# Folding four more blocks of an out-projection, with the row moves issued by GpSimd

## The chip, the cores and the metric

The kernel runs on one core of a Trainium2 chip. The metric is the device time of one execution in microseconds (us), the median of several runs. Engines are named as in the profile: PE is TensorE (PEld its weight loads), DVE is VectorE, ACT is ScalarE, POOL is GpSimd, SP is SyncE, which here only issues transfers.

## The reference

Four layers follow each other on `x` of 2048 tokens by 448 numbers (bf16): attention, gated MLP, attention, gated MLP. Each adds to `x` what it computes from the layer-normed `x`.

```
def _A_ref(x, wqkv, wo):                      # 16 heads of 28, window of 8 keys, two tokens apart
    q, k, v = split(x @ wqkv)
    logits = q . k[pos - 2*(0..7)] * 28**-0.5     # masked where the position is negative
    o = softmax(logits) @ v
    return o.reshape(B, S, 448) @ wo              # the out-projection
def _B_ref(x, w_gate, w_up, w_down):
    return ((x @ w_gate) * (x @ w_up)) @ w_down   # 448 -> 1792 -> 448
x = x + _A_ref(layernorm(x), A_wqkv, A_wo);  x = x + _B_ref(layernorm(x), ...)
x = x + _A_ref(layernorm(x), A_wqkv, A_wo);  x = x + _B_ref(layernorm(x), ...)
```

## The kernel before

Tokens lie in 16 blocks of 128 (even tokens first, then odd ones). The layers are numbered 0 to 3; 0 and 2 are attention, 1 and 3 the MLP. Everything stays in SBUF; attention and MLP of neighbouring layers overlap, chunk by chunk.

**Work on PE.** The matmuls of the projections contract 64 rows at a time, and two of them run side by side on the two halves of PE's rows. Such a *pair* is two rows of the profile that start together (helper `pair`, line L353: 64 rows, 128 columns of weights, 256 to 512 columns of data). Scores (L838) and attention times V (L873) are bursts of many small matmuls, 64 rows by 32 columns (64 by 64 in the first groups). Between the halves of a burst, a pair may be written as eight strips of 32 columns (line L356, tiles `64*32`), so that PE keeps its small shape through the burst.

**Out-projection.** `attn_back` makes the attention outputs of 120 tokens, `norm` (L901 to L914) divides by the softmax sum and writes `oT`: 16 heads stand in 512 rows (4 chunks of 128), each head 28 rows and 4 pad rows. `y_blocks(li, B)` multiplies two blocks B and B+1 with `wo_g` by `twin_blocks`: 8 pairs, or 16 matmuls, in two parts of 4 pairs each. `x_block` (DVE, L946) adds the result to `x_sb`.

**Fold.** 448 of the 512 rows hold numbers. For blocks from `FOLD[li]` on, the last two heads (rows 64 to 127 of chunk 3) are moved by DMA into the pad rows of the other chunks: four moves `mv`, 3 or 4 rows by 4 rows, 512 or 1024 bytes each, then one move `mw` that copies rows 0 to 63 of chunk 3 of the odd blocks to rows 64 to 127, since the second block of a pair needs them on the other half. Seven pairs are then enough. The weights are folded once in the same way (`wf` 0 to 3 from DRAM, then `wf` 4 within SBUF), after the last unfolded out-projection and before the first folded one. In layer 2 all blocks are folded, in layer 0 those from 10 on. `GROUPS` says how many blocks share one set of moves.

**Order.** Nothing is scheduled at run time. `ORDER` gives, for each engine, the numbers of the operations one after the other, and `BANKS` the PSUM banks; both are tables that were found by a search outside of the file. An entry `a+b*c` means that bursts a and b are cut up between strips of operation c. `emit` puts a semaphore wait ahead of an operation that needs another engine's result; what stands behind it on the same engine waits too. Transfers are issued by SP in the order of its row (`plain_dma`, L446, and the transposes L608 and L735).

Of the kernel before, what the change touches and what calls it, by code (L numbers as in the profile page):

```python
# [8 lines left out]
D = 448  # L9
H = 16  # L10
DH = 28
# [3 lines left out]
NBLK = S // 128  # L15
NCH = S // 512
QB = 120
NQB = 17
# [15 lines left out]
FOLD = {0: 10, 2: 0}  # L34
# [63 lines left out]
def grp_nc(g):  # L98
# [56 lines left out]
    ),  # L155
    "pool": (
        "24 18 28 29 25 39 40 32 33 35 41 26 20 22 21 30 27 36 19 31 34 42 37 43 44 68 66 38 77 23 76"
    ),
# [223 lines left out]
def build(nc, A_x, A_wqkv, A_wo, B_w_gate, B_w_up, B_w_down, out):  # L382
# [10 lines left out]
    bf = dt.bfloat16  # L393
# [524 lines left out]
    def y_blocks(li, B, prio):  # L918
        bk = Banks(2)
# [208 lines left out]
```

## Time and profile before

| | |
|---|---|
| median of 3 runs | 380.81 us (380.18 to 380.89) |
| the profiled execution | 380.47 us, span 378.7 us |
| PE busy | 373.6 us, 99% of the span |
| DVE, ACT, POOL busy | 285.4, 200.0, 7.8 us |
| granted clock of PE | 1.00 |
| matmuls on `wo_g` in whole pairs (L353) | 228 rows, 349 ns each |
| transfers `oT<-oT` issued by SP | 40, median 638 ns of SP each |

A matmul's row in the profile is longer than the step to the next one, since matmuls are pipelined: what a pair costs is read from the start of one row of the timeline to the start of the next, not from the duration of an instruction. The timeline's rows name start, length, engine, line and operation, the tiles as out<-in with partitions x elements, the count, and in brackets the idle time before. In the list of waits a row gives engine, line and tile, what it waited for, and then the total in us, the number of times and the longest.

### The profile page before, as it was taken

What the parts mean: (1) busy time and instruction counts of PE and PEld (TensorE: products, weight loads), DVE (VectorE), ACT (ScalarE), POOL (GpSimd) and SP (SyncE); (2) the same over time, 40 slices, a digit from 0 to 9 for tenths busy, and PEclk for the clock granted to TensorE, in tenths of its full rate; (3) what the DMA queues carried; (4) which work ended last, traced back from release to release, by engine and by line L of the source; (5) the groups of instructions that cost most, each with busy time, mean ns of one, the idle gap of its engine ahead of it and who ended that gap; (6) DMA issues with size and microseconds to landing.
All of it is one profiled execution on the core that took longest, in us unless ns stands there. A gap on an engine that the chain in (4) does not pass through costs nothing.

```text
span 378.7 us, 14371 instructions
## 1 busy us (share of the span) xinstructions
PE 373.6 (99%) x6376; PEld 208.7 (55%) x6376; DVE 285.4 (75%) x647; ACT 200.0 (53%) x384; POOL 7.8 (2%) x35
## 2 busy tenths in 40 slices
PE   8999999999999999999999999999999999999997
PEld 3645577644554445544676666645555444445764
DVE  7998999999867953878698598559699778446324
ACT  4897895778715355246548215638647533043310
POOL 6000000000000000000000000000000000000000
PEclk9999999999999999999999999999999999999999
DMA  7665544500250216312104123510106102312002
GB/s 260 167 163 144 112 113 95 81 10 13 31 86 5 58 28 93 43 28 50 25 10 64 27 29 63 93 31 5 29 12 102 35 5 54 74 42 70 2 2 85
DMA packets 56401, 23.10 MB, mean 61 GB/s; under 512 B 46004, under 2 KB 56324, under 8 KB 56340
## 3 DMA queue, kind: packets, MB, share of 16 engines
q1 hardware_dynamic: 56196, 22.14, 28.1%
q8 instruction: 50, 0.82, 0.9%
q14 instruction: 11, 0.09, 0.1%
q10 hardware_dynamic: 144, 0.06, 0.1%
HBM read 8.59 MB, written 2.71 MB: 30 GB/s over the span
## 4 chain that ended last, share of the span: by engine, by line
PE 96%; ACT 2%; POOL 1%; DVE 1%; issue 0%; DVEq 0%; POOLq 0%
PE ps L353 86%; PE ps L356 4%; PE ps L838 2%; PE ps L873 2%; PE ps L997 1%; POOL hT L493 1%; ACT E_sb L848 1%; PE ps L619 0%; PE ps L515 0%; ACT xnTa L626 0%; ACT qk L715 0%; DVE Qz L826 0%; PE ps L615 0%; ACT v_sb L807 0%; ACT xnTa L629 0%
## 5 line engine op out<-in xcount | busy, mean ns | idle before, releaser
L353 PE MATMUL ps<-xnTb,WGU 64*128 64x512 bf16 (+1 forms) x1898 | 173.3, 332 | 0.0
L353 PEld LDWEIGHTS ps<-xnTb,WGU 64*128 64x128 bf16 x1898 | 91.4, 94 | 71.2 <-DVE hT L985 0.6
L982 ACT ACTIVATE g_sb<-ps 128x512 bf16<-128x512 f32 (+1 forms) x140 | 68.9, 509 | 92.4 <-PE ps L353 88.4
L985 DVE TENSOR_TENSOR hT<-g_sb,ps 128x512 bf16<-128x512 bf16 (+1 forms) x140 | 77.4, 573 | 38.2 <-ACT g_sb L982 37.3
L353 PE MATMUL ps<-WD,hT 64*128 64x448 bf16 x786 | 80.8, 349 | 0.0
L353 PEld LDWEIGHTS ps<-WD,hT 64*128 64x128 bf16 x786 | 37.4, 94 | 32.4 <-DVE hT L985 0.2
L353 PE MATMUL ps<-xnTa,WQK 64*128 64x512 bf16 (+1 forms) x490 | 52.1, 352 | 0.0
L946 DVE TENSOR_TENSOR x_sb<-x_sb,ps 128x448 bf16<-128x448 bf16 x62 | 36.6, 611 | 16.4 <-PE ps L353 16.3
L848 ACT ACTIVATE E_sb<-ps,shift_sb 128x1024 bf16<-128x1024 f32 (+1 forms) x36 | 37.9, 1071 | 14.2 <-PE ps L838 13.8
L605 DVE TENSOR_SCALAR xn_sb<-x_sb,mv,rstd 128x896 bf16<-128x896 bf16 (+1 forms) x64 | 35.0, 568 | 6.6 <-ACT rstd L589 5.8
L584 DVE BATCH_NORM_STATS2 st<-x_sb 128x6 f32<-128x448 bf16 x64 | 38.5, 615 | 1.0 <-DMA x_sb<-in_A_x_dram 0.7
L353 PEld LDWEIGHTS ps<-xnTa,WQK 64*128 64x128 bf16 x490 | 23.1, 94 | 20.9 <-DVE WQK L523 0.3
L715 ACT ACTIVATE qk<-ps 128x1024 bf16<-128x1024 f32 (+1 forms) x28 | 25.4, 931 | 14.2 <-PE ps L353 12.0
L902 ACT ACTIVATE R_sb<-R_sb 128x480 f32<-128x480 f32 (+1 forms) x34 | 20.4, 603 | 13.7 <-DVE R_sb L901 13.6
L855 DVE TENSOR_TENSOR E_sb<-E_sb,MK 128x1024 bf16<-128x1024 bf16 (+1 forms) x36 | 23.4, 655 | 4.6 <-ACT E_sb L848 4.6
L914 DVE TENSOR_TENSOR oT<-O_sb,R_sb 128x480 bf16<-128x480 f32 (+5 forms) x38 | 22.2, 600 | 5.3 <-ACT R_sb L903 5.3
L353 PE MATMUL ps<-wo_g,oT 64*128 64x448 bf16 x228 | 25.6, 349 | 0.0
L353 PE MATMUL ps<-WV,xnTa 64*128 64x336 bf16 (+3 forms) x252 | 23.0, 304 | 0.6 <-DVE O_sb L891 0.2
L901 DVE STREAM_SHUFFLE R_sb<-O_sb 128x480 f32<-128x480 f32 (+1 forms) x34 | 23.2, 691 | 0.0
L826 DVE TENSOR_SCALAR Qz<-qk,qmask 128x960 bf16<-128x960 bf16 (+1 forms) x36 | 14.7, 451 | 7.5 <-ACT qk L715 6.5
L903 ACT ACTIVATE R_sb<-R_sb 128x480 f32<-128x480 f32 (+1 forms) x34 | 20.0, 602 | 0.4
L587 ACT ACTIVATE lnv<-mv,eps_sb 128x2 f32<-128x2 f32 (+2 forms) x31 | 8.9, 293 | 19.1 <-DVE mv L586 19.1
(63 smaller groups left out, 221.0 us busy)
## 6 DMA issues: line engine op xcount, KB each, us to landing
out_dram<-x_sb SPq DMA_DIRECT2D x15, 112.0 KB, 1.8
x_sb<-in_A_x_dram SPq DMA_DIRECT2D x3, 448.0 KB, 5.6
hT<-in_A_wqkv_dram SPq DMA_DIRECT2D x4, 224.0 KB, 4.6
WGU<-in_B_w_gate_dram SPq DMA_DIRECT2D x4, 224.0 KB, 3.7
WGU<-in_B_w_up_dram SPq DMA_DIRECT2D x4, 224.0 KB, 4.3
WD<-in_B_w_down_dram SPq DMA_DIRECT2D x2, 448.0 KB, 4.0
WGU<-in_B_w_gate_dram SPq DMA_DIRECT2D x2, 336.0 KB, 4.6
WGU<-in_B_w_up_dram SPq DMA_DIRECT2D x2, 336.0 KB, 4.6
```

Source lines behind the costliest of these rows:

```text
L353: return lambda E: E.matmul(out(), lhs(), rhs(), start=start, stop=stop)
L584: sc.add("dve", one(lambda E, B=B: E.bn_stats(st6[:, B, :], x_sb[:, B, :]), ("bn", li, B)), 525.0, deps=[("x", li - 1, B)] + ([("xn", li - ...
L605: sc.add("dve", one(lambda E, B=B, dst=dst, src=src: E.tensor_scalar(dst, src, mv[:, B, 0:1], rstd[:, B:B + 1], ALU.subtract, ALU.mult), ( ...
L715: return E.activation(dst, src, ACT.Copy) if hasattr(E, "activation") else E.tensor_copy(dst, src)
L848: return E.activation(E_sb[:, slot, 2 * hp:2 * hp + 2, 0:w], ps[:, b0:b0 + 2, 0:w], ACT.Exp, bias=shift_sb[:, 0:1], scale=SCALE)
L855: return E.tensor_tensor(e, e, MK[:, kind, 0:nc].unsqueeze(1).unsqueeze(1).to_broadcast([128, 2, w // nc, nc]), ALU.min)
L901: sc.add("dve", one(lambda E: E.stream_shuffle(R_sb[:, rs, 0:w], O_sb[:, os_, 0:w], [DH] * 32), ("Rs", li, qb)), dve_est(w) + 20.0, deps=[ ...
L902: sc.add("act", one(lambda E: E.activation(R_sb[:, rs, 0:w], R_sb[:, rs, 0:w], ACT.Ln), ("Rl", li, qb)), act_est(w, False), deps=[("Rs", l ...
L914: return E.tensor_tensor(oT[:, :, (a + 256) % HALF:(a + 256) % HALF + z - a], O[:, :, a - tok:z - tok], R_sb[:, rs, 0:w].rearrange("p (h n ...
L946: sc.add("dve", one(lambda E: E.tensor_tensor(x_sb[:, B, :], x_sb[:, B, :], ps[:, bk[w], 0:D], ALU.add), ("x", li, B)), dve_est(D), deps=[ ...
L982: sc.add("act", one(lambda E, gs=gs, bk=bk: E.activation(g_sb[:, gs, 0:nt], ps[:, bk[0], 0:nt], ACT.Copy), ("G", li, j, fc)), act_est(nt), ...
L985: sc.add("dve", one(lambda E, gs=gs, bk=bk, fc=fc: E.tensor_tensor(hT[:, fc, hs, 0:nt], g_sb[:, gs, 0:nt], ps[:, bk[1], 0:nt], ALU.mult), ...
```

## The change

`FOLD` for layer 0 goes from 10 to 6, so blocks 6 to 9 (two more calls of `y_blocks`) take 7 pairs in place of 8. The moves `mv`, `mw` and `wf` are issued by POOL (`"pool"` in place of `"sp"`). `mw` writes to a new tile `oU` in place of rows 64 to 127 of `oT`, and therefore waits for the attention outputs and for two of the four `mv` (before, it waited for all four); the out-projection waits for all five. The tables `ORDER` and `BANKS` are new: up to the first attention groups of layer 0 they are as they were, behind that they differ on every engine.

```diff
-FOLD = {0: 10, 2: 0}
+FOLD = {0: 6, 2: 0}
...
+    oU = sb([128, 4, 128], bf, "oU")
...
             if B == G:
                 a = 128 * ((B + 2) % 8)
                 for j, row, m, _, _ in PADS:
-                    plain_dma("sp", oT[32 * j + DH:32 * j + 32, 0:m, a:a + 128 * n], oT[row:row + 4 * m, 3, a:a + 128 * n], ("mv", li, B, j), f"d_m{li}_{B}", deps=norms(B, B + n), prio=prio - 0.1)
-                odd = [oT[lo:lo + 64, 3, a:a + 128 * n].rearrange("p (b w) -> p b w", w=256)[:, :, 128:256] for lo in (64, 0)]
-                plain_dma("sp", odd[0], odd[1], ("mw", li, B), f"d_m{li}_{B}", deps=[("mv", li, B, j) for j in range(4)], prio=prio - 0.1, mode=1)
-            nd = nd + [("mw", li, G)]
+                    plain_dma("pool", oT[32 * j + DH:32 * j + 32, 0:m, a:a + 128 * n], oT[row:row + 4 * m, 3, a:a + 128 * n], ("mv", li, B, j), f"d_{'mw'[j > 1]}{li}_{B}", deps=norms(B, B + n), prio=prio - 0.1)
+                odd = [oU[64:128, a // 256:a // 256 + n // 2, :], oT[0:64, 3, a:a + 128 * n].rearrange("p (b w) -> p b w", w=256)[:, :, 128:256]]
+                plain_dma("pool", odd[0], odd[1], ("mw", li, B), f"d_w{li}_{B}", deps=norms(B, B + n) + [("mv", li, B, 0), ("mv", li, B, 1)], prio=prio - 0.1, mode=1)
+            nd = nd + [("mw", li, G)] + [("mv", li, G, j) for j in range(4)]
...
-                    plain_dma("sp", wo_g[32 * j + DH:32 * j + 32, 0:m, :], ...
-                plain_dma("sp", wo_g[64:128, 3, :], wo_g[0:64, 3, :], ("wf", 4), "d_wf", ...
+                    plain_dma("pool", wo_g[32 * j + DH:32 * j + 32, 0:m, :], ...
+                plain_dma("pool", wo_g[64:128, 3, :], wo_g[0:64, 3, :], ("wf", 4), "d_wf", ...
...
     "pool": (
-        "24 18 28 29 25 39 40 32 33 35 41 26 20 22 21 30 27 36 19 31 34 42 37 43 44 68 66 38 77 23 76"
+        "24 18 28 29 25 39 40 32 33 35 41 26 20 22 21 30 27 36 19 31 34 42 37 43 44 68 66 38 77 23 76 432 430 429 431 424 433 425 426 427 428 564 561 562 563 "
...
```

Three places of the new order follow.

POOL, which issued no transfer before, at the moves of blocks 10 to 13 of layer 0 (rows of the changed kernel; `oT<-oT` are `mv`, `oU<-oT` is `mw`; the brackets name the semaphores waited for, `sem_dve` here for the attention outputs):

```order
L447 DMA oT<-oT 4x4x256 [waits sem_dve]
L447 DMA oT<-oT 4x4x256
L447 DMA oT<-oT 4x4x256 [waits sem_dve]
L447 DMA oU<-oT 64x128 [waits sem_d_m0_10]
L447 DMA oT<-oT 4x3x256
L447 DMA oT<-oT 4x4x256
L447 DMA oT<-oT 4x3x256 x2
L447 DMA oU<-oT 64x128 [waits sem_d_m0_12]
L447 DMA oT<-oT 4x3x256
```

The moves of blocks 12 and 13 are mixed into those of 10 and 11: the third row waits for the later outputs, and the eight transfers from there on stand behind that wait. On SP the same moves stood, in the kernel before, as follows:

```order
L446 DMA wo_g<-wo_g 64x448 [waits sem_d_wf]
L446 DMA oT<-oT 4x3x256 [waits sem_dve]
L446 DMA oT<-oT 4x4x256 x2
L446 DMA oT<-oT 64x128 [waits sem_d_m0_10]
L446 DMA oT<-oT 4x3x256
L446 DMA oT<-oT 64x128 [waits sem_d_m0_12]
```

PE, at the out-projections that need these moves (rows of the changed kernel from the last of a stretch of MLP down-projections, `WD,hT`, on):

```order
L353 MATMUL ps<-WD,hT 128x448 x56
L353 MATMUL ps<-xnTb,WGU 128x512 x84
L353 MATMUL ps<-wo_g,oT 128x448 x7
L353 MATMUL ps<-wo_g,oU 128x448
L353 MATMUL ps<-wo_g,oT 128x448 x7
L353 MATMUL ps<-wo_g,oU 128x448
L353 MATMUL ps<-wo_g,oT 128x448 x12
L353 MATMUL ps<-xnTb,WGU 128x512 x56
```

The two out-projections, of blocks 12 and 10, now stand together behind 84 MLP matmuls; before, 56 down-projection and 56 MLP matmuls preceded them, and MLP matmuls lay between their parts.

PE, at a place near the front, before:

```order
L873 MATMUL ps<-E_sb,v_sb 32x64 x32
L353 MATMUL ps<-xnTb,WGU 128x256 x28
L873 MATMUL ps<-E_sb,v_sb 32x64 x32
L353 MATMUL ps<-xnTb,WGU 128x256 x56
L353 MATMUL ps<-wo_g,oT 128x448 x8
```

and in the changed kernel:

```order
L874 MATMUL ps<-E_sb,v_sb 32x64 x64
L353 MATMUL ps<-xnTb,WGU 128x256 x84
L353 MATMUL ps<-wo_g,oT 128x448 x8
L353 MATMUL ps<-xnTb,WGU 128x256 x14
L353 MATMUL ps<-wo_g,oT 128x448 x8
```

Two bursts with MLP pairs between them became one burst.

More of the change, by code (lines that the diff above doesn't have):

```diff
@@ L138 @@
         "148 166 154 183 161 184 167 45 185 165 163 156 157 46 151 210 170 188 173 159 73 78 172 71 74 72 75 190 191 179 246 193 215 181 176 216 178 251 270 219 "
[16 rows of a table removed]
[16 rows of a table added]
     ),
     "pool": (
-        "24 18 28 29 25 39 40 32 33 35 41 26 20 22 21 30 27 36 19 31 34 42 37 43 44 68 66 38 77 23 76"
+        "24 18 28 29 25 39 40 32 33 35 41 26 20 22 21 30 27 36 19 31 34 42 37 43 44 68 66 38 77 23 76 432 430 429 431 424 433 425 426 427 428 564 561 562 563 "
+        "565 590 591 648 594 593 649 651 592 652 650 680 678 679 677 681 844 847 846 845 848 997 996 999 998 1000 1217 1216 1218 1219 1220 1404 1403 1401 1402 "
+        "1405 1454 1455 1458 1457 1456"
     ),
     "sp": (
[7 rows of a table removed]
[5 rows of a table added]
     ),
@@ L433, in build @@
     sem_names += [f"d_t{li}_{j}" for li in range(4) for j in range(len(CH[li]))]
-    sem_names += [f"d_p{li}_{j}" for li in (0, 2) for j in range(len(CH[li]))] + [f"d_v{q}" for q in range(NQB)] + ["d_one", "d_stv", "d_wf"] + [f"d_m{l}_{b}" for l in (0, 2) for b in range(0, NBLK, 2)]
+    sem_names += [f"d_p{li}_{j}" for li in (0, 2) for j in range(len(CH[li]))] + [f"d_v{q}" for q in range(NQB)] + ["d_one", "d_stv", "d_wf"] + [f"d_{k}{l}_{b}" for k in "mw" for l in (0, 2) for b in range(0, NBLK, 2)]
     vt_all = nc.dram_tensor("vt", (256, S), bf, kind="Internal").ap()
@@ L936, in y_blocks @@
                 for j, _, m, h, d in PADS:
-                    plain_dma("sp", wo_g[32 * j + DH:32 * j + 32, 0:m, :], A_wo[DH * h + d:DH * h + d + 4 * m, :].rearrange("(r c) d -> r c d", c=m), ("wf", j), "d_wf", deps=WO + war, prio=prio - 0.2)
-                plain_dma("sp", wo_g[64:128, 3, :], wo_g[0:64, 3, :], ("wf", 4), "d_wf", deps=[("wf", j) for j in range(4)], prio=prio - 0.2, mode=1)
+                    plain_dma("pool", wo_g[32 * j + DH:32 * j + 32, 0:m, :], A_wo[DH * h + d:DH * h + d + 4 * m, :].rearrange("(r c) d -> r c d", c=m), ("wf", j), "d_wf", deps=WO + war, prio=prio - 0.2)
+                plain_dma("pool", wo_g[64:128, 3, :], wo_g[0:64, 3, :], ("wf", 4), "d_wf", deps=[("wf", j) for j in range(4)], prio=prio - 0.2, mode=1)
             nd = nd + [("wf", 4)]
-        twin_blocks(lambda w: ps[:, bk[w], 0:D], lambda w, c, lo: oT[lo:lo + 64, c, 128 * ((B + w + 2) % 8):128 * ((B + w + 2) % 8) + 128], lambda w, c, lo: wo_g[lo:lo + 64, c, :],
+        twin_blocks(lambda w: ps[:, bk[w], 0:D], lambda w, c, lo: oU[64:128, (B + 2) % 8 // 2, :] if fold and (c, lo) == (3, 64) else oT[lo:lo + 64, c, 128 * ((B + w + 2) % 8):128 * ((B + w + 2) % 8) + 128], lambda w, c, lo: wo_g[lo:lo + 64, c, :],
                     (("Y", li, B), ("Y", li, B + 1)), [range(4)], [[]], nd + WO, prio, bk, short=int(fold))
```

122 rows, old and new, of tables (BANKS, ORDER) are left out of this document.

## The prediction

> **What bounds the kernel now.** I read the page first: busy times, the slices and the chain that ended last.
>
> ```profile
> PE 373.6 (99%) x6376; PEld 208.7 (55%) x6376; DVE 285.4 (75%) x647; ACT 200.0 (53%) x384; POOL 7.8 (2%) x35
> PE   8999999999999999999999999999999999999997
> POOL 6000000000000000000000000000000000000000
> PE 96%; ACT 2%; POOL 1%; DVE 1%; issue 0%; DVEq 0%; POOLq 0%
> ```
>
> PE has work in 99% of the span and is 96% of the chain; POOL is empty behind the first slice. A busy PE could still be a slow one, since the ends of matmuls are modelled. So I read the timeline of PE for the step from one pair to the next, at the folded out-projections of layer 0 and at two bursts:
>
> ```profile
> 118.77 1.68 PE L353 MATMUL ps<-wo_g,oT 64*128 64x448 bf16 x16
> 120.28 1.68 PE L353 MATMUL ps<-xnTb,WGU 64*128 64x512 bf16 x14
> 121.79 0.73 PE L353 MATMUL ps<-wo_g,oT 64*128 64x448 bf16 x6
> ...
> 49.16 1.71 PE L353 MATMUL ps<-xnTb,WGU 64*128 64x256 bf16 x28
> 50.80 0.32 PE L873 MATMUL ps<-E_sb,v_sb 64*32 64x64 bf16 x32
> 51.05 3.23 PE L353 MATMUL ps<-xnTb,WGU 64*128 64x256 bf16 x56
> 54.12 0.92 PE L353 MATMUL ps<-wo_g,oT 64*128 64x448 bf16 x8
> ...
> 91.30 0.25 PE L873 MATMUL ps<-E_sb,v_sb 64*32 64x64 bf16 x16
> 91.37 0.40 PE L356 MATMUL ps<-xnTb,WGU 64*32 64x512 bf16 x8
> 91.59 0.21 PE L873 MATMUL ps<-E_sb,v_sb 64*32 64x64 bf16 x8
> ```
>
> Eight pairs of 448 columns take 120.28 - 118.77 = 1.51 us, 0.189 us a pair; seven of 512 take 1.51 us, 0.216 us a pair; 28 of 256 (51.05 to 54.12) 0.110 us a pair. These steps repeat without holes, so PE has hardly a wait to give up: a gain must come from less work on PE. And since PE is never ahead, whatever comes late for it adds to the time in full.
>
> **The change, part by part.**
>
> *Fewer pairs.* Blocks 6 to 9 are two calls of `y_blocks`, each one pair shorter: 2 x 0.189 = **-0.38 us**, on the path.
>
> *Fewer changes of shape.* From 49.16 to 50.80, 14 pairs take 1.64 us where 14 x 0.110 = 1.54 would do: 0.10 more for going over to the small shape. The burst of 32 takes 51.05 - 50.80 = 0.25 us; inside a run of strips 16 take 91.37 - 91.30 = 0.07, so 32 would take 0.14: 0.11 more. A stay in the small shape thus costs 0.21 us beside its matmuls. Counted along PE's rows of the two orders, there are 40 stays before and 38 after: 2 x 0.21 = **-0.42 us**. Between 0 (if the saved time is waited away) and this I take the whole, since the steps show no waits. Five more pairs are written as strips; eight strips of 512 take 91.59 - 91.37 = 0.22, as the pair does: nothing.
>
> *One wait near the front.* The new order also begins to differ here:
>
> ```profile
> 43.74 0.70 PE L873 MATMUL ps<-E_sb,v_sb 64*32 64x64 bf16 x64
> 44.74 0.64 PE L838 MATMUL ps<-Qz,qk 64*64 64x128 bf16 x32 [0.30 <-ACT qk L715]
> 45.63 0.60 PE L353 MATMUL ps<-WV,xnTa 64*128 64x336 bf16 x6 [0.24 <-DVE O_sb L891]
> ```
>
> The scores wait for ACT and the V projection behind them for DVE. After, half of that V projection stands ahead of the scores. ACT's operations up to the awaited one are as long as before, so the scores start no earlier; at most the second wait goes. Between 0 and -0.24 I take **-0.1 us**.
>
> *The moves on POOL.* Here the change can lose. What the moves cost on SP, and what stands around them:
>
> ```profile
> L446 SPq DMA_DIRECT2D oT<-oT x40: 531/638/783, 98.9 to 315.5; - x40
> SPq L446 <- DMA oT<-oT: 6.6, 5, 1.6
> 206.04 1.31 SPq L608 DMA_TRANSPOSE xnTb<-xn_sb  x1
> L946 DVE TENSOR_TENSOR x_sb<-x_sb,ps 128x448 bf16<-128x448 bf16 x62 | 36.6, 611 | 16.4 <-PE ps L353 16.3
> L914 DVE TENSOR_TENSOR oT<-O_sb,R_sb 128x480 bf16<-128x480 f32 x28 | 18.0, 651 | 1.7 <-ACT R_sb L903 1.7
> L982 ACT ACTIVATE g_sb<-ps 128x512 bf16<-128x512 f32 x84 | 48.3, 593 | 61.2 <-PE ps L353 58.1 <-DVE hT L985 1.4 <-DVE mv L586 0.8
> L985 DVE TENSOR_TENSOR hT<-g_sb,ps 128x512 bf16<-128x512 bf16 x84 | 55.5, 680 | 20.6 <-ACT g_sb L982 20.3 <-PE ps L353 0.2
> L605 DVE TENSOR_SCALAR xn_sb<-x_sb,mv,rstd 128x512 bf16<-128x512 bf16 x32 | 12.6, 405 | 3.4 <-ACT rstd L589 2.5 <-DMA xnTb<-xn_sb 0.7
> ```
>
> A move takes SP 0.64 us to issue. The five `mw` waited 6.6 / 5 = 1.3 us (longest 1.6) for the moves issued just ahead of them: the time to land. Call POOL's time for one issue p and the landing l = 1.3. No row shows a transfer issued by POOL. The nearest is SP's 0.64 for the same transfers, the short end 0.53; as the long end I take SP's dearest kind near by, a transpose at 1.31. The right row is the wrong engine, so I take the middle of 0.64 and 1.31, **p = 0.97**, and keep 0.53 to 1.31 for the range.
>
> How much time is there? I go through the sets of moves in the new order, from the operation that feeds the last attention output to the first matmul that needs the moves, by the steps above:
>
> - *Blocks 12 and 10 of layer 0.* On DVE the output (L914) stands right behind the add (L946) that waits for the 42nd of the 56 `WD,hT` matmuls of the PE rows in the section on the change. From there PE has 7 x 0.189 + 42 x 0.216 = 10.4 us of work to the first `wo_g` matmul. The add takes 0.61, the output (cut in two) some 0.75: 9.0 us are left. Behind the wait POOL issues eight transfers, and the last has to land: 8p + l. It fits up to p = 0.96.
> - *Blocks 6 to 9 of layer 2.* PE has 8.9 us of work between the MLP unit on which the last output's DVE row depends and the out-projection. ACT 0.59, DVE 0.68 and 0.65 leave 7.0 us for five issues: fits up to p = 1.14.
> - *Blocks 6 and 7 of layer 0,* the first folded ones now. From the end of their last attention burst PE has 16.2 us of work (before: 7.3 us to this unfolded projection). The output needs some 8 us of that: in the kernel before the same burst ended at 66.2 and the output at 72.2, and it now stands two DVE rows further back. POOL issues the four moves, the second half of the weight fold and `mw`: 6p + l against 8.1, fits up to 1.13. The weight fold itself starts when the projection of blocks 4 and 5 is done, 16.4 us ahead.
>
> ```profile
> 65.87 0.31 PE L873 MATMUL ps<-E_sb,v_sb 64*32 64x64 bf16 x32
> 71.00 1.23 DVE L914 TENSOR_TENSOR oT<-O_sb,R_sb 128x480 bf16<-128x480 f32 x2
> ```
>
> All other sets have 8.5 us or more for five issues. So POOL makes PE late by 8(p - 0.96) + 5(p - 1.14) + 6(p - 1.13), each where positive. At p = 0.97 that is 0.1; a landing of 1.6 adds 0.3 at the first place. I take **+0.2 us**. At p = 1.2 it is 1.9 + 0.3 + 0.4 = 2.6, at 1.31 some 4.7; at 0.64 nothing.
>
> The Trainium skill ("DMA: Bandwidth & Descriptors", section "SWDGE vs HWDGE vs iDMA") says that a core of GpSimd computes the descriptors of a transfer issued there, and its "Specifications" give about 1 us to the first byte against about 0.6 us from SP; added as 0.4 to SP's 0.64 its price would be p = 1.04, an estimate from that page, lateness 0.6 us and a time of 380.5. No run here shows it yet.
>
> *What SP no longer does:* 40 moves x 0.64 = 26 us and the weight fold. PE's waits show nothing that came late from SP, so nothing is gained. `oU` costs no instruction: the same matmuls read another tile.
>
> Sum: -0.38 - 0.42 - 0.1 + 0.2 = -0.7 us. The profiled execution took 380.47 (span 378.7), so 379.77 of its kind; it lay 0.34 below the median of 380.81, and for the median I get **380.1 us**, 0.19% less. What differs by under 0.2%, 0.76 us, a measurement of this kernel can hardly tell from no change; that line lies at 380.05.
>
> **The rivals.**
>
> *POOL is the new wait.* If an issue takes 1.2 us or more, out-projections of three places wait 2.6 us and more: 380.81 - 0.9 + 2.6 = 382.5, slower. It decides from p = 1.12 on, where lateness (1.3) eats the 0.9 and gives no change, and from about 1.18 by over 0.2%. For it: three places fit with little to spare, and PE forgives nothing. Against: the same move takes SP 0.64. Chance 0.22.
>
> *VectorE holds POOL up.* In the 9.0 us of the first place DVE runs three layer-norm writes (L605, 0.41 us each). If POOL cannot write descriptors while one runs, the eight issues stretch by up to 1.2 us: with p = 0.97 lateness 1.3, time 380.81 - 0.9 + 1.3 = 381.2, within the line; alone, with p = 0.64, it stays hidden (8 x 0.64 + 1.2 + 1.3 = 7.6 of 9.0). Before, POOL issues nothing, so the trace speaks neither way. Chance 0.08. The rule is the Trainium skill's, "SBUF — State Buffer", section "Who interferes with whom".
>
> *The order does not deliver.* The rows of the new order may wait for ACT, DVE or PSUM banks where the old ones did not; every engine's row is new behind 43 us. Two bursts' worth of such waits (2 x 0.45) gives back all: 380.8. For it: DVE is busy 75%, and from 50 to 70 us all the time (third number of the table by stretches):
>
> ```profile
> 50.00:60.00 10.00, 10.00 (x219) 7.91 (x217) 10.00 (x27) 8.85 (x21) 0.00 (x0) 1.00 0.42 109
> 60.00:70.00 10.00, 10.00 (x192) 6.70 (x188) 10.00 (x26) 5.78 (x15) 0.00 (x0) 1.00 0.57 106
> ```
>
> Against: the distances from the scores to the exponentials and back are no shorter than before. Chance 0.08.
>
> **How the numbers follow.** My forecast (p up to about 1.1, lateness 0 to 1.2) has 0.62: times from 379.7 to 381.1, of which 0.35 lie under 380.05 and 0.27 within the line. POOL late: 0.20 slower, 0.02 same. VectorE: half within, half (with a dearer p) over. The order: 0.01, 0.02, 0.05. Faster 0.36, same 0.35, slower 0.29. The range goes from 379.5 (the whole 0.24 at the front, and no lateness: 380.81 - 1.04 = 379.8, less 0.3 for the runs' spread) to 383.0 (p = 1.2 with a landing of 1.6).
>
> **What would show it.** In the profile after: 230 matmuls on `wo_g`, strips included as quarters; the steps 0.189, 0.216 and 0.110 as before; POOL's rows give p. If POOL's issue is near 0.97, PE stands still for at most some tenths of a us ahead of the out-projection of blocks 12 and 10, and nowhere else. I am wrong if POOL takes over 1.12 us, if a wait on PE ends by ACT or DVE for over 0.5 us in a place that had none, or if the stays in the small shape cost the same in total.

## The result and the profile after

The changed kernel takes 380.03 us (median of 20 runs, 379.45 to 380.94), the kernel before 380.81 (20 runs, 379.97 to 381.44). The ratio is 0.9985, 95% interval 0.9978 to 0.9992: 0.57 us less, between 0.3 and 0.84. The profiled execution took 380.03 us, span 378.2.

The page after: busy times and POOL's slices.

```profile
PE 373.3 (99%) x6402; PEld 210.7 (56%) x6402; DVE 286.1 (76%) x647; ACT 201.5 (53%) x384; POOL 40.0 (11%) x90
POOL 6100002330104020000300300000300303000000
```

PE is as full as before. POOL now works where its slices were empty. The instructions on the tiles `oT` and `oU` that POOL issues (least, median and most ns of one), its waits, and the time from the start of an issue to the landing:

```profile
L447 POOL DMA_DIRECT2D oT<-oT x40: 570/587/817, 72.5 to 320.6; - x40
L447 POOL DMA_DIRECT2D oU<-oT x10: 557/562/619, 76.5 to 319.5; - x10
POOL oU L447 <- DMA oT<-oT: 11.3, 9, 2.0
DMA to landing us min/median/max: 1.7/2.1/4.5
```

An issue takes POOL 0.59 us, not 0.97. The landing is not clearly longer than SP's: `mw` waits 11.3 / 9 = 1.26 us in the mean for the moves ahead of it, and 2.0 at most (SP: 1.3 and 1.6). For SP's moves the profile records no landing.

For the whole I use one stretch of PE: from the start of the burst of scores near 39 us, where the two orders are still the same, to the start of PE's last run, which is the same in both. Its two ends, first before (38.96 to 370.86), then after (38.82 to 370.31):

```profile
38.96 0.64 PE L838 MATMUL ps<-Qz,qk 64*64 64x128 bf16 x32
370.86 5.50 PE L997 MATMUL ps<-WD,hT 128*128 128x224 bf16 x42
```

```profile
38.82 0.64 PE L839 MATMUL ps<-Qz,qk 64*64 64x128 bf16 x32
370.31 5.50 PE L998 MATMUL ps<-WD,hT 128*128 128x224 bf16 x42
```

331.90 and 331.49 us: in this pair of profiles the change is worth 0.41 us. That is little more than the folded pairs, and less than the ratio (0.57) and the medians (0.78) say. The experiments look for what else there is.

### The profile page after: what moved, and what is told of

It reads as the page before. It is cut to its first block, busy times and chain, and to the rows that moved or that the text cites. A ratio compares the mean times of both kernels' runs of the same rounds, so it can differ in the third digit from the quotient of the medians.

```text
span 378.2 us, 14468 instructions
## 1 busy us (share of the span) xinstructions
PE 373.3 (99%) x6402; PEld 210.7 (56%) x6402; DVE 286.1 (76%) x647; ACT 201.5 (53%) x384; POOL 40.0 (11%) x90
## 4 chain that ended last, share of the span: by engine, by line
PE 95%; DVE 2%; DMA 1%; ACT 1%; issue 0%; SPq 0%; DVEq 0%
PE ps L353 85%; PE ps L356 4%; PE ps L839 2%; PE ps L874 2%; PE ps L998 1%; DMA x_sb<-in_A_x_dram 1%; ACT E_sb L849 1%; DVE xn_sb L606 0%; PE ps L620 0%; SPq L447 0%; DVE st L585 0%; ACT qk L716 0%; DVE Qz L827 0%; ACT v_sb L808 0%; DVE O_sb L888 0%
## 5 line engine op out<-in xcount | busy, mean ns | idle before, releaser
L353 PE MATMUL ps<-xnTb,WGU 64*128 64x512 bf16 (+1 forms) x1878 | 170.2, 332 | 0.0
L353 PEld LDWEIGHTS ps<-xnTb,WGU 64*128 64x128 bf16 x1878 | 92.4, 94 | 69.0 <-issue 0.6
L983 ACT ACTIVATE g_sb<-ps 128x512 bf16<-128x512 f32 (+1 forms) x140 | 69.7, 510 | 107.0 <-PE ps L353 96.3
L353 PE MATMUL ps<-WD,hT 64*128 64x448 bf16 x802 | 82.1, 349 | 0.0
L353 PEld LDWEIGHTS ps<-WD,hT 64*128 64x128 bf16 x802 | 39.0, 94 | 32.9 <-ACT E_sb L849 0.3
L447 POOL DMA_DIRECT2D oT<-oT x40 | 23.7, 596 | 213.3 <-DVE oT L915 204.1
L888 ACT ACTIVATE O_sb<-ps 128x512 f32<-128x512 f32 (+3 forms) x23 | 12.1, 546 | 10.4 <-PE ps L874 10.3
```

The costliest lines, as they stand in the source:

```text
L353: return lambda E: E.matmul(out(), lhs(), rhs(), start=start, stop=stop)
L447: sc.add(q, one(lambda E: E.dma_start(dst, src), key), {"sp": 520.0, "act": 500.0, "pool": 1000.0}[q], deps=deps, dma=sem, mode=mode, prio ...
L983: sc.add("act", one(lambda E, gs=gs, bk=bk: E.activation(g_sb[:, gs, 0:nt], ps[:, bk[0], 0:nt], ACT.Copy), ("G", li, j, fc)), act_est(nt), ...
```

## Experiments

Times are medians; the ratio is against the kernel before on the same chip. Where an expectation gives the stretch to PE's last matmul (336.7, 337.1), it ends 5.2 us later than the stretch above, in the same run.

### The fold by itself

```diff
                 chunks = chunks[:len(chunks) - (short and flip)]
+                if again and flip:
+                    chunks = [0, 1, 1, 2]
...
+                    ... short=int(fold), again=li == 0 and B in (6, 8))
```

> The changed kernel with an eighth pair again in the two out-projections of layer 0's blocks 6 to 9 (one pair of the second part is done twice, so these blocks get a wrong sum). If the fold is worth its pairs, because PE has hardly a wait to hide them in: 380.03 + 2 x 0.19 = 380.4 us. If the gain came from the order alone and the pairs lay beside a wait: 380.0. In the profile: the stretch from PE's burst of scores near 39 us to PE's last matmul grows by 0.38, or by nothing.

380.53 us, ratio 0.9999 (0.9991 to 1.0008), against 0.9985 for the changed kernel. In the profile the stretch is 331.78 us (38.93 to 370.71): 0.29 more than the changed kernel's first. The changed kernel's second profile (below), which like this one lacks the wait near 324 us that the third experiment deals with, has 331.45: against it the two pairs cost 0.33 of the 0.38. The fold is worth its pairs.

### The moves on POOL by themselves

```diff
-                    plain_dma("sp", oT[32 * j + DH:32 * j + 32, 0:m, ...      # the kernel before: mv, mw, wf
+                    plain_dma("pool", oT[32 * j + DH:32 * j + 32, 0:m, ...
```

> The kernel before with the moves and the weight fold issued by GpSimd in the order in which SP issued them; nothing else differs. POOL's issue took 0.59 us in the changed kernel and what it issued some 2.0 us to land (SP: 0.64 and 1.3 to 1.6). By these numbers every set still lands ahead of its out-projection (the tightest, blocks 12 and 10 of layer 0, at some 117.8 us for 118.8), so no change: 380.8 +- 0.2. If GpSimd's moves disturb the rest (VectorE, transfers): 381.2 or more. If freeing SP was worth something: 380.4 or less.

380.62 us, ratio 1.0000 (0.9992 to 1.0009). Changing the engine alone costs and brings nothing that this interval, 0.35 us to either side, could show. PE's timeline showed something else, at a place 11 us ahead of the first transfer that POOL issues:

```profile
74.64 0.73 PE L343 MATMUL ps<-WV,xnTa 64*128 64x336 bf16 x8
75.62 2.55 PE L343 MATMUL ps<-xnTb,WGU 64*128 64x512 bf16 x22 [0.25 <-DMA xnTb<-xn_sb]
```

Four pairs that need 4 x 0.142 = 0.57 us are followed by the next run only after 0.98: PE waited 0.4 us for a transpose. In the first profile of the kernel before the two rows are 0.57 apart, without a wait:

```profile
74.75 0.73 PE L353 MATMUL ps<-WV,xnTa 64*128 64x336 bf16 x8
75.32 2.97 PE L353 MATMUL ps<-xnTb,WGU 64*128 64x512 bf16 x26
```

### The late moves at 320 us

The changed kernel has a place that the prediction did not name, the set of blocks 14 and 15 of layer 2. PE, POOL and SP there, and the time to landing of the last two moves:

```profile
324.20 0.73 PE L353 MATMUL ps<-WD,hT 64*128 64x448 bf16 x6
324.97 0.36 PE L353 MATMUL ps<-wo_g,oT 64*128 64x448 bf16 x2
...
319.45 0.56 POOL L447 DMA_DIRECT2D oU<-oT  x1 [1.65 <-DMA oT<-oT]
320.01 1.20 POOL L447 DMA_DIRECT2D oT<-oT  x2
...
318.21 6.43 SPq L609 DMA_TRANSPOSE xnTb<-xn_sb  x4
...
oT<-oT POOLq DMA_DIRECT2D x2, 6.0 KB, 4.4
```

Three pairs of 0.189 take 0.77 us: PE stood still for 0.20. Two of the four `mv` stand behind `mw` and its wait, so they were issued at 320 us. The four transposes of SP run at the same time, and the two moves took a median of 4.4 us from issue to landing in this window, where those of the whole run take 1.9 to 2.4. The edit, in POOL's order:

```diff
-1454 1455 1458 1457 1456      # mv mv mw mv mv
+1454 1455 1457 1456 1458      # mv mv mv mv mw
```

> The changed kernel with one line of POOL's order changed: in the set of blocks 14 and 15 of layer 2 all four mv stand ahead of mw, where two stood behind it. In the profile of the changed kernel PE stood still for 0.20 us ahead of this out-projection (near 324.4 us), with the last two moves issued at 320 us and four transposes running from 318.2 to 324.6. If these late moves are what PE waited for: the stillness goes, 380.03 - 0.20 = 379.8. If PE waited for mw, or for something else: it stays, 380.0.

379.81 us, ratio 0.9980 (0.9972 to 0.9989). The stretch is 331.34, and PE reaches the projection without a wait. The two moves, now issued by 318.97, took 2.0 us to land. To see whether this is more than chance, both were run again side by side:

> The changed kernel once more, for a second profile. If what the first pair of profiles shows is the change and not the chance of one execution: PE's stretch from the scores at 38.8 us to its last matmul is 336.7 us again (before: 337.1), with the wait of 0.20 us near 324.4. If it is chance: it differs from 336.7 by more than 0.15.

> The kernel with all four mv first once more, side by side with the changed one. By the late moves: the stretch is 0.15 to 0.2 us shorter than the changed kernel's, no wait near 324.4, and its time 0.1 to 0.2 us under it, 0.7 to 0.8 under the kernel before. By chance: no order between the two.

380.10 us (0.9985, 0.9975 to 0.9995) for the changed kernel and 379.97 (0.9980, 0.9972 to 0.9989) with the moves first. The stretch is 331.45 us (39.22 to 370.67) and 331.37 (38.91 to 370.28). But the changed kernel has no wait at 324 us this time, so that expectation was half wrong. Of the five profiles with the changed kernel's order at this place (its own two, the fold by itself, the two bursts and the six more moves below) two show the wait, with 0.20 and 0.33 us; of the three with the moves first, none. It is a wait that comes and goes, and its removal is worth some 0.1 us on the mean, which the times leave open. The version with the moves first had the shortest stretch and the lowest median both times; by how much it is faster than the changed kernel, these runs don't show.

### The kernel before once more

> The kernel before once more, for a second profile. In the profile of the old order with moves on POOL, PE waited 0.4 us at 75 us for a transposed xnTb, before POOL had issued any move; in the first profile of the kernel before it did not. If this wait comes and goes with the old order's transposes: the stretch from the scores to the last matmul is between 337.1 and 337.6, with 0 to 0.4 us of standing still at 75 us. If POOL's moves made it: 337.1 and none.

380.61 us, ratio 0.9998 (0.9989 to 1.0007). PE at 75 us and at 292:

```profile
74.22 0.73 PE L353 MATMUL ps<-WV,xnTa 64*128 64x336 bf16 x8
75.16 3.20 PE L353 MATMUL ps<-xnTb,WGU 64*128 64x512 bf16 x28 [0.21 <-DMA xnTb<-xn_sb]
...
290.18 1.88 PE L353 MATMUL ps<-WD,hT 64*128 64x448 bf16 x18
292.21 0.39 PE L353 MATMUL ps<-xnTb,WGU 64*128 64x512 bf16 x2
```

0.94 us for four pairs of 0.142 is a wait of 0.37, and 2.03 for nine pairs of 0.189 one of 0.33, both ahead of the first use of a transposed `xnTb`. The stretch is 332.59 (38.40 to 370.99), longer than the expectation's upper end would allow (332.4). So the kernel before has two places where PE arrives just as transposes land. The three profiles of its order, with the one where POOL issues the moves, have 331.90, 332.59 and 332.42 us (mean 332.30); the two of the changed kernel 331.49 and 331.45 (mean 331.47). None of the eight profiles with the new order, other than the one with SP's moves below, has a wait at 75 us. That the new order is free of this wait is likely from these eleven profiles, not proven. The difference of the means is 0.83 us, near the 0.78 of the medians. But in the later comparison the medians lie only 0.45 us apart (380.55 and 380.10), and the ratio is 0.9985 both times, 0.57 us: with so few profiles, 0.83 is a rough figure.

### What a stay in the small shape costs

```diff
-387 388 310 313      # PE: burst, burst, 7 pairs, 7 pairs
+387 310 313 388      # burst, 14 pairs of 256 columns, burst
```

> The changed kernel with the burst of 64 attention matmuls at 48.7 us cut in two again, 14 MLP pairs between the halves, as before the change. By the prediction a stay in the small shape costs 0.21 us beside its matmuls: 380.03 + 0.21 = 380.24, and the stretch of PE from this burst to the first out-projection behind it (5.26 us) grows by 0.21. By the rival, that one bare burst of 64 is itself slower than two of 32 (0.68 against 0.32 + 0.25 us in the two profiles): the stretch grows by 0.02 +- 0.03, and the time stays at 380.0.

380.41 us, ratio 0.9992 (0.9983 to 1.0000). The stretch from the burst to the first projection, in the changed kernel and with two bursts:

```profile
48.72 0.70 PE L874 MATMUL ps<-E_sb,v_sb 64*32 64x64 bf16 x64
49.40 4.76 PE L353 MATMUL ps<-xnTb,WGU 64*128 64x256 bf16 x84
53.98 0.35 PE L353 MATMUL ps<-wo_g,oT 64*128 64x448 bf16 x1
```

```profile
48.57 0.34 PE L874 MATMUL ps<-E_sb,v_sb 64*32 64x64 bf16 x32
49.12 1.72 PE L353 MATMUL ps<-xnTb,WGU 64*128 64x256 bf16 x28 [0.21 <-ACT R_sb L903]
50.78 0.34 PE L874 MATMUL ps<-E_sb,v_sb 64*32 64x64 bf16 x32
51.05 3.44 PE L353 MATMUL ps<-xnTb,WGU 64*128 64x256 bf16 x56
54.30 0.54 PE L353 MATMUL ps<-wo_g,oT 64*128 64x448 bf16 x3
```

5.26 and 5.73 us: neither theory's number, because the edit brought waits. 0.21 is named in the row; the 28 pairs from 51.05 on took 3.25, against 3.07 for the same rows before the change: 0.18 more. What is left of the 0.47 is 0.08. The kernel before has the same two bursts without these waits, from 48.84 to 54.12: 5.28, 0.02 more than one burst. So one burst in place of two bare ones (bursts without strips) saves 0.02 to 0.08, not 0.21. The longer burst is the dearer one: 0.68 for 64 matmuls, against 0.32 + 0.25 in the kernel before.

Two bursts between strips, with 7 pairs taken out from between them, in the version with the moves first:

```diff
-1417+1418*1313/4/3 1321 1435+1436*1314/5
+1321 1417+1418*1313/4/3 1435+1436*1314/5
```

> The kernel with all four mv first (380.03 - 0.2), and in it 7 MLP pairs that stood between two bursts cut up between strips (near 286.7 us: attention times V, 7 pairs, scores) stand ahead of both, so that the two stays in the small shape become one; nothing else differs. Read from PE's timeline, from the start of the WD,hT run ahead of the first burst (282.68 us) to the start of the run behind the second (289.54): 6.86 us now. By the prediction (0.21 us for a stay beside its matmuls): 6.65. If only the way into the small shape is saved, and the burst's own excess stays (0.10 each by the profiles): 6.76. If a stay costs nothing: 6.86. The out-projection behind may get its moves up to 1 us later, so the whole time is not the measure: 379.6 to 380.6.

380.90 us, ratio 1.0008 (0.9997 to 1.0018): about 1 us more than the version with the moves first. PE with the moves first, and with one stay:

```profile
280.97 4.70 PE L353 MATMUL ps<-WD,hT 64*128 64x448 bf16 x48
289.54 1.88 PE L353 MATMUL ps<-WD,hT 64*128 64x448 bf16 x18
```

```profile
280.98 6.27 PE L353 MATMUL ps<-WD,hT 64*128 64x448 bf16 x62
289.97 0.23 PE L839 MATMUL ps<-Qz,qk 64*32 64x64 bf16 x8 [0.76 <-DVE O_sb L892]
290.61 1.69 PE L353 MATMUL ps<-WD,hT 64*128 64x448 bf16 x16
```

The same work takes 8.57 and 9.63 us. The second half of the scores now waits for VectorE to empty PSUM. The start ahead of it is at 288.83, so 1.14 us for a step of some 0.18: 0.96. The pairs that were moved ahead wait 0.23 near 285. Without the two, 1.06 turns into -0.13: about 0.13 us saved, nearer to the way in alone (0.10) than to 0.21. The seven pairs between the bursts were the time in which PSUM was emptied.

The timelines also allow a sum over all stays behind the front, from the burst at 48.8 us on. For each stay I take the time from its first matmul to the next pair, less the steps of the pairs that its strips stand for; its way in is what the step ahead of it takes over the usual one. In the first profile of the kernel before, 30 stays take 12.17 us inside and 2.93 for the ways in; in that of the changed kernel, 27 stays take 12.21 and 2.57. Together that is 15.10 to 15.15 us in the three profiles with the old order and 14.74 to 14.85 in the six whose stays are the changed kernel's. So fewer stays save about 0.3 us in the whole, all of it in the ways in.

### How much room POOL had

```diff
+    scr = sb([128, 192], bf, "scr")
+    for i in range(6):
+        plain_dma("pool", scr[16 * i:16 * i + 16, :], WV[0:16, 0, 0:192], ("more", i), "d_more", deps=[("wv", 0)])
```

> The changed kernel with six more transfers issued by POOL (16 rows of 384 bytes, to a place that nothing reads) behind the wait of the set of blocks 12 and 10 of layer 0, so 14 issues stand behind it in place of 8. In the changed kernel the last of them was issued by 117.7 us and needed some 2 us to land, for an out-projection at 121.26: 1.6 us to spare. Six issues of 0.59 take 3.5 us. If POOL's issue is on this path as the prediction has it, and PE pays lateness in full: 3.5 - 1.6 = 1.9 us of standing still ahead of that out-projection, and 380.03 + 1.9 = 381.9. If PE has other waits to lose later: less than 1 us in the whole. If the transfers disturb each other: more than 2.5.

381.02 us, ratio 1.0013 (1.0003 to 1.0023). The out-projection of blocks 12 and 10 on PE, and POOL ahead of it; then both in the changed kernel:

```profile
111.77 9.23 PE L353 MATMUL ps<-xnTb,WGU 64*128 64x512 bf16 x84
122.22 0.91 PE L353 MATMUL ps<-wo_g,oT 64*128 64x448 bf16 x7 [1.23 <-issue]
...
112.79 2.95 POOL L447 DMA_DIRECT2D scr<-WV  x6
...
119.65 0.61 POOL L447 DMA_DIRECT2D oT<-oT  x1
```

```profile
121.26 0.92 PE L353 MATMUL ps<-wo_g,oT 64*128 64x448 bf16 x7
...
112.65 0.57 POOL L447 DMA_DIRECT2D oT<-oT  x1 [8.93 <-DVE O_sb L892]
...
117.40 0.61 POOL L447 DMA_DIRECT2D oT<-oT  x1 [0.34 <-issue]
```

42 pairs of 0.216 us from 111.77 on would end at 120.84, and PE goes on at 122.22: it stands still for 1.38 us (1.23 in the bracket, since a row is longer than its step). The stretch is 332.72 (38.36 to 371.08), 1.25 more than the changed kernel's 331.47. The wait carries the name "issue": none of the events that the profile shows ended it. The last move fits: issued at 119.65, it took 2.5 us and landed at 122.1. In the changed kernel it was issued at 117.40 and landed 1.9 us later, 2.0 ahead of 121.26. The expected 1.9 was too much: there were 2.0 us to spare and not 1.6, and the six took 0.49 each, not 0.59. Counted from the start of the 84 matmuls (111.77, and 112.19 in the changed kernel), the last move was issued 2.67 us later and took 0.6 longer to land; less the 2.0, that is 1.3. The mechanism stands: lateness of POOL is PE's, in full, once the room is used up.

### What the order is for

The changed kernel with the old tables for PE, ACT, DVE and the banks, and SP's old row without the moves:

> The changed kernel (blocks 6 to 9 folded, moves on POOL) with the tables of the kernel before on PE, ACT, DVE and for the banks, operation for operation; POOL issues in the changed kernel's order, SP in the old one without the moves. If the new order's part is to give the new moves their time: in the old order the output of blocks 6 and 7 ends at 72.2 us and their projection starts at 72.8; five issues, the landing ahead of mw (2 us) and of mw itself (2 us) take some 7 us, so PE stands still for 6 to 7 us there and the time is 386 to 387. If the new order only saves changes of shape, and the fold would do in the old one too: 380.8 - 0.4 = 380.4.

393.4 us, ratio 1.0327 (1.0240 to 1.0414). The waits of PE were as expected at the first place, and came at blocks 8 and 9 as well:

```profile
79.06 1.65 PE L354 MATMUL ps<-wo_g,oT 64*128 64x448 bf16 x7 [6.03 <-DMA oU<-oT]
...
91.00 1.25 PE L354 MATMUL ps<-xnTb,WGU 64*128 64x512 bf16 x10
95.28 1.67 PE L354 MATMUL ps<-wo_g,oT 64*128 64x448 bf16 x7 [3.03 <-DMA oU<-oT]
```

9.1 us of waits do not make the 15.4 by which this profiled execution (395.43 us; the three runs go from 390.13 to 395.43) is longer than that of the changed kernel. The table by stretches (the window, its length, PE's busy time and so on; the granted clock stands third from the end):

```profile
79.00:81.00 2.00, 1.94 (x12) 1.01 (x14) 0.00 (x0) 0.00 (x0) 0.00 (x0) 0.50 0.09 21
83.00:85.00 2.00, 2.00 (x16) 1.00 (x14) 1.97 (x5) 0.00 (x0) 0.00 (x0) 0.65 0.00 0
...
99.00:101.00 2.00, 2.00 (x12) 0.62 (x10) 1.97 (x6) 1.11 (x1) 0.00 (x0) 0.50 0.00 0
```

After the first wait PE works at a clock of 0.50 for some 5 us, after the second (95.28) for some 6. Half the clock for 11 us costs half of that, so waits and clock together make 14.6 of the 15.4. The Trainium skill ("TensorE: Matmul & The Clock Gate", Part 1) has half the clock after an idle window of about 3.4 us. The trace agrees: the second wait, 3.03 in the bracket, is 3.4 us from the start of the last pair ahead of it (91.00 + 4 x 0.216) to 95.28.

The changed kernel with the moves on SP, in its row where POOL issued them by time:

```diff
-                    plain_dma("pool", oT[32 * j + DH:32 * j + 32, 0:m, ...
+                    plain_dma("sp", oT[32 * j + DH:32 * j + 32, 0:m, ...
```

> The changed kernel with moves and weight fold issued by SP again, put into its row where POOL issued them by time (0.64 us each there, landing 1.3 to 1.6). If GpSimd is needed because SP's row is full of transposes between 62 and 78 us: the ten transfers for blocks 6 and 7 end some 4 us later, PE stands still ahead of the out-projection at 80.3 us, and the time is 383 to 386. If SP has room (its waits held nothing up before): 380.0 +- 0.3.

388.98 us, ratio 1.0235 (1.0204 to 1.0265). SP's row, and the projection of blocks 6 and 7:

```profile
81.05 1.10 SPq L736 DMA_TRANSPOSE v_sb<-vt  x1
82.20 0.59 SPq L447 DMA_DIRECT2D oU<-oT  x1
...
84.11 1.65 PE L353 MATMUL ps<-wo_g,oT 64*128 64x448 bf16 x7 [3.87 <-DMA oU<-oT]
```

The wait is the 4 us expected. The time is longer than the 383 to 386 expected: a clock of 0.50 follows for some 5 us, and PE waits 1.7 and 1.4 us at two later out-projections. So in the places tried, the fold of blocks 6 to 9 needs both other parts of the change: the order gives the moves time, and POOL a queue without transposes. Other places for the moves in SP's row were not tried.

## Why the prediction came out

The forecast of 380.1 against 380.03 was right in its total. That is partly luck: a wait that the working had left out made up for terms that did not come in full.

- *Fewer pairs, -0.38:* right; the profile after has the 230 matmuls on `wo_g` that were forecast, strips counted as quarters.
- *Fewer changes of shape, -0.42:* 0.3. The price of a stay was too large and the count too small. Behind the front PE's two orders hold three stays fewer, not two (30 and 27; the front has one more, hence 40 and 38), and they save 0.1 us each, not 0.21. The step that failed is the 0.11 that a bare burst takes over the rate of its matmuls between strips: it was taken as a cost that goes with the stay, and the time inside the stays is the same, 12.17 and 12.21 us.
- *The wait near the front, -0.1:* nothing. The idle time in the brackets fell from 0.54 to 0.22 us,

```profile
45.37 1.18 PE L353 MATMUL ps<-xnTa,WQK 64*128 64x256 bf16 x14 [0.22 <-DVE O_sb L892]
46.39 0.73 PE L353 MATMUL ps<-WV,xnTa 64*128 64x336 bf16 x8
```

  but seven pairs take 46.39 - 45.37 = 1.02 us here, where 7 x 0.110 = 0.77 would do, and the V projection between the bursts makes one more stay. The way from the scores at 38.96 to the burst at 48.84 takes 9.88 us before; after, from 38.82 to 48.72, 9.90.
- *POOL, +0.2:* of the right size by luck. The price p was taken at 0.97 and is 0.59; the landing of 1.3 was good. The 9.0 us worked out for blocks 12 and 10 was good too: from the wait's end at 112.65 to PE's 121.26 are 8.6, of which the moves need 6.6, to the last landing at 119.25. None of the three named places waits. The lateness came at blocks 14 and 15 of layer 2, 0.2 us in one profile and none in another. For this set the prediction counted 8.5 us or more; 8.3 were there (316.64 to 324.97), and the wait of `mw` in the middle and a landing of 4.4 beside the transposes used them up.
- *No waits to give up:* the gap in the working. One profile of the kernel before showed steps without holes, and the prediction took them for the kernel. Two further profiles of that order had waits of 0.4 us at 75 us, and one of these 0.33 at 292, 0.37 in the mean of the three. The new order showed neither.

Together, in the means of the stretch: -0.38 - 0.32 - 0.37 + 0.1 = -0.97 us. Measured are -0.83; the rest is in steps of under 0.1 each.

Of the rivals, POOL as the new wait fell with p = 0.59. (By the prediction's own formula lateness eats the 0.9 at p = 1.07 and passes it by 0.2% at 1.15, not at 1.12 and 1.18.) VectorE holding POOL up is small: in the changed kernel

```profile
74.26 0.82 POOL L447 DMA_DIRECT2D oT<-oT  x1
74.12 0.85 DVE L827 TENSOR_SCALAR Qz<-qk,qmask 128x960 bf16<-128x960 bf16 x2
```

is the one move that took 0.82, where the median is 0.59; the profiles of its order have 0.75 to 0.82 at this place each time. It is 0.2 us in a set whose last transfer was issued at 76.49 and landed 1.9 us later, for PE at 80.31. The Trainium skill's rule ("SBUF — State Buffer", section "Who interferes with whom") fits there, though no run isolates it. It does not show beside the writes of `xn_sb` that the prediction feared: moves issued beside these took 0.57 to 0.61. The Trainium skill's price for a transfer issued by GpSimd ("DMA: Bandwidth & Descriptors", "Specifications") does not show in the issue, 0.59 against SP's 0.64, where the prediction's sentence added it. Whether the landing holds it stays open: from the end of the last issue to PE's start are 1.96 us in the run with six more moves, and 1.32 in the run with the moves on SP; but the mean waits of `mw` are 1.26 and 1.3. The order that would not deliver did not come about.

## What to carry over

One profile shows where a kernel waits in that execution; where a transfer lands just as it is needed, take a second before calling an engine free of waits. Count an engine's issue and the landing behind it as two prices: here an issue took 0.59 us, and from its start to the landing it was 1.7 to 4.5. And work taken from between two bursts may have been the time in which something else was emptied.

## What was not expected of the hardware

A wait of PE costs more than its length once it is long: after 3.0, 3.9 and 6.0 us of standing still (by the brackets) the granted clock was 0.50 for some 5 to 6 us. After the 1.23 us of the run with six more moves it stayed at 1.00:

```profile
122.20:126.00 3.80, 3.78 (x40) 2.22 (x42) 2.86 (x6) 0.00 (x0) 0.00 (x0) 1.00 0.41 71
```

And small moves land late beside transposes: beside four of them two moves of 6 KB took 3.5 to 4.6 us in the five profiles with the changed kernel's order at that place, and 2.0 to 2.1 in the three that issue them ahead of the transposes.
